# One operand item per half step, a second hand-out of side work in two MLP blocks, and other barriers inside the transform

## The chip, the cores and the metric

The kernel runs on one core of a Trainium2 chip. The metric is device time in microseconds of one launch; the median of three runs is given, and one further execution was recorded by the profiler. TensorE does the matrix products and transposes, VectorE and ScalarE move and combine what it leaves in PSUM, GpSimd and SyncE issue most transfers.

## The reference, cut to what matters

Three stages follow one another on `(4, 576, 512)` float32 data: attention with random features, a mixer (a token MLP and a channel MLP), and a block that adds a two-dimensional Fourier transform, normalizes and applies a second channel MLP.

```
# mixer, channel part; u has 4 x 576 rows of 512, w_ch1 is 512 x 1536
h2 = np.maximum(u @ w_ch1, 0.0) @ w_ch2
x = u + h2
# second block; w_ch1 is 512 x 2048
X = np.fft.fft(x, axis=1)
X = np.fft.fft(X, axis=2)
u = x + np.real(X)
mu = np.mean(u, axis=-1, keepdims=True)
var = np.mean((u - mu) ** 2, axis=-1, keepdims=True)
un = (u - mu) / np.sqrt(var + 1e-06)
out = u + np.maximum(un @ w_ch1, 0.0) @ w_ch2
```

## The kernel before

**Products.** Every operand is a sum of a high and a low part, and each product is three TensorE passes (high by high, high by low, low by high). A matmul has up to 512 columns.

**The first channel MLP** (`ch_block`, `mlp`) runs over five blocks of 512 rows, `at_` 0 to 4, in 12 steps each. A step is `up` (12 matmuls into a bank H, L775), `relu` (ScalarE writes hh, VectorE writes hl, L863 and L864) and `down` of the step before (12 matmuls into four banks A, L901). A block ends with eight additions on VectorE (L907).

**Side work.** Everything else is cut into items of a planned cost in microseconds and stands in two lists, `side.lead` and `side.rest`. `Side.step(budget)` adds its budget to a credit (at most 4.6), then hands out items from `lead` and after it from `rest` while the credit pays. A `None` is a barrier: it ends the list for this call. `side.later(fn, n)` puts an issue off by n calls. `side.until` takes items at once until a condition holds, whatever their cost. Handing out means that the instructions are written behind what has been written so far, in the queue of each engine; each engine then works through its own queue in that order. In `mlp` a step has one such call behind `down`, or with `twice` two with half the budget each, one ahead of `down` and one behind it. Before the change only the last MLP block `ff_block(0)` (matmuls L775 and L1285, 16 steps) has `twice`.

**What the lists hold.** From block 3 on, `lead` holds the transforms `dft(0)` to `dft(3)`, one for each batch. One transform is even0 to even4 (sums on VectorE; even4 ends with L983), s1e0 to s1e2 (matmuls L1055 to L1057 into a bank S, read out by `put`), odd0 to odd3, s1o0 to s1o2 (L1065, L1066; L1043 and L1044 read out the last), and for each of two row groups `both` (two banks S, L1082), plus and minus (`spectrum`, L1088 to L1090, read the two banks), and two nat (four transposes L1095 and one addition L1096 each), at last left0 and left1. There are two banks S, used in turn: whatever needs a third waits until the first has been read. `rest` holds the splitting of weights (`widen`: take, rest, size, high, low, unit, scaled at L371, then a store), in block 4 the first normalization `norm(0)` and the pair sums `sum_pairs`: eight times a load (L1222), `add` (L1227), `sums` (L1233 to L1236), a cast by ScalarE into a buffer `so` (L1242), `low` (L1246) and two stores (L420). Two buffers `so` serve in turn.

**Operand items.** When `rest` is empty, `begin_ff` opens the operands of the paired MLP, and the items of `prepare_early` (b11, b12, b22, b21, each for q = 0 and 1) transpose normalized rows `un` into a bank S (L1332) and split them (L1325, L1326).

**The paired MLP** (`paired_block`, L1507 and L1520) has eight steps of four products; `pace` hands out side work after each with a budget of 1.6 and a credit of at most 2.0, but not after the first two. Its second half, 16 slabs of nine matmuls, needs `reopen`, which stands in `lead` behind `dft(3)`: `side.until` forces it. From slab 4 on, it prepares the operands of the next paired block, which read the rows of `norm(2)` (stats L1165 and L1166, root, sqrt L1176, newton L1180 to L1185, `un` L1194); `side.until` forces those too.

Of the kernel before, what the change touches and what calls it, by code (L numbers as in the profile page):

```python
# [25 lines left out]
NCH, NFF = DCH // 128, DFF // 128  # L26
# [7 lines left out]

SLOT0_US, SLOT1_US, SLOT_US, FIRST_US, SHORT_US, CH_US, LAST_US, FF_US, S_US, SAVED_US = 1.2, 0.45, 1.2, 3.9, 1.2, 4.3, 4.9, 5.2, 1.6, 4.6


NP = NFF // 2  # L40
# [150 lines left out]
def pieces(t0, n):  # L191

    done = 0
    while done < n:
        b, s = divmod(t0 + done, S)
        step = min(n - done, S - s)
        yield done, step, b, s
        done += step
# [103 lines left out]
def mix_kernel(ctx: ExitStack, tc: tile.TileContext, qt, kt, va, om, w1, w2, wch, wff, t1, t2, out):  # L302
# [142 lines left out]
    def bank(tag):  # L445
        if tag not in pools:
            tag = "A"
        if tag == "A" and spare:

            tag = spare.pop(0)  # L450
            spare.append(tag)
        pl, bufs = pools[tag]
        return pl.tile([128, 512], F32, tag=tag, name=tag, bufs=bufs)
# [238 lines left out]
    for b in range(B):  # L692
# [4 lines left out]
        c = [("k", i, g) for i in range(kn, ke) for g in range(2)]  # L697
# [11 lines left out]
    early = []  # L709
# [18 lines left out]
    def turns(n, c):  # L728
        return list(range(n)) if c % 2 == 0 else list(range(n))[::-1]
# [19 lines left out]
    def halves(t, h):  # L749
        return t[:, 0, 512 * h:512 * h + 512], t[:, 1, 512 * h:512 * h + 512]  # L750
# [4 lines left out]
    def ch_cols(c):  # L755
        return min(BLK, NTOK - c * BLK)
# [12 lines left out]
    def up(w, uh, ul, n):  # L769

        hb = bank("H")
        c = 0
        for kk in range(4):
            for a, u in ((0, uh), (0, ul), (1, uh)):
                pe.matmul(out=hb[:, 0:n], lhsT=w(a, kk), rhs=u[:, kk, 0:n],  # L775
                          start=(c == 0), stop=(c == 11))
                c += 1
        return hb
# [81 lines left out]
    def relu(hb, n):  # L860
        hh = hp.tile([128, BLK], F32R, tag="hh", name="hh")[:, 0:n]
        hl = hp.tile([128, BLK], F32R, tag="hl", name="hl")[:, 0:n]
        act.activation(out=hh, in_=hb[:, 0:n], func=AF.Relu)  # L863
        dve.scalar_tensor_tensor(out=hl, in0=hb[:, 0:n], scalar=0.0, in1=hh, op0=ALU.max, op1=ALU.subtract)  # L864
        return hh, hl

    def mlp(steps, first_of, u, cols, down, budget, prepare, twice=False):


        prev = None  # L870
        for i, x in enumerate(steps):
            hb = mlp0.pop("hb") if "hb" in mlp0 else up(first_of(x), *u, cols)
            h = relu(hb, cols)
            last = i == len(steps) - 1
            if last:
                for fn in prepare[:1]:
                    fn()
            elif twice:
                side.step(budget / 2)
            if prev is not None:  # L880
                down(*prev)
            prev = i, x, h
            if not last:
                if fill:
                    fill.pop(0)()
                side.step(budget / 2 if twice else budget)
        for fn in prepare[1:]:
            fn()
        down(*prev)

    def ch_block(at_, c, u, prepare, budget):
        acc = [bank("A") for _ in range(4)]
        cols = ch_cols(c)

        def down(n, j, h):
            hi, lo = halves(mix.get(j), 1)
            hh, hl = h
            for c_, (a, v) in enumerate(((hi, hh), (lo, hh), (hi, hl))):
                for i in range(4):
                    cs = slice(i * 128, i * 128 + 128)  # L900
                    pe.matmul(out=acc[i][:, 0:cols], lhsT=a[:, cs], rhs=v, start=(n == 0 and c_ == 0),  # L901
                              stop=(n == NCH - 1 and c_ == 2))
            mix.used()
        mlp(turns(NCH, at_), ch_first, u, cols, down, budget, prepare)
        for i in range(4):
            for off, n, b, s in pieces(c * BLK, cols):
                dve.tensor_tensor(out=x2[b][:, i, s:s + n], in0=acc[i][:, off:off + n], in1=x2[b][:, i, s:s + n],  # L907
                                  op=ALU.add)

    u = mlp0["u"]  # L910
# [6 lines left out]
    u = u2  # L917
# [21 lines left out]
    U = [None] * B  # L939
# [7 lines left out]
    def dft(b):  # L947

        st = {}
        x = x2[b]  # L950
# [141 lines left out]
        def nat(u, src):  # L1092
            pb = bank("S")
            for c in range(4):
                pe.transpose(pb[:, c * 128:c * 128 + 128], src(c), ident)  # L1095
            dve.tensor_tensor(out=u, in0=pb, in1=u, op=ALU.add)  # L1096

        def rows(r):
            def both():
                if r == 0:  # L1100
                    U[b] = (xp if b else xu).tile([128, 4, 512], F32, tag="x2", name="U", padded_shape=[128, 4, S])
                e_ps, st["o"] = bank("S"), bank("S")
                stage2(e_ps, 0, st["ch"], 0, r)
                stage2(st["o"], 0, st["sh"], 1, r)
                st["e"] = f2.tile([128, 257], F32, tag="e", name="e", bufs=2)
                act.copy(out=st["e"], in_=e_ps[:, 0:257])

            def plus():
                spectrum(U[b][:, r], st["e"], st["o"], False)
                if r == 0:  # L1110
                    act.copy(out=st["e"][0:1], in_=st["alt"][:, 0:257])

            def minus():
                spectrum(U[b][:, 2 + r], st["e"], st["o"], True)

            return [(0.0, both), (0.9, plus), (0.9, minus),
                    None, (0.65, lambda: nat(U[b][:, r], lambda c: x[:, c, r:r + 256:2])),
                    (0.65, lambda: nat(U[b][:, 2 + r], lambda c: x[:, c, 288 + r:544 + r:2])), None]

        pr, po = b // 2, 64 * (b % 2)  # L1120

# [15 lines left out]
        def left1():  # L1137
            spectrum(L[pr][po:po + 64], st["e"][po:po + 64], st["o"][po:po + 64], False)
            if po:
                nat(L[pr], lambda c: gath[pr][:, c, :])  # L1140

        return ([(1.7, even0), (1.6, even1), (1.1, even2), (1.2, even3), (1.1, even4), None]
                + [(0.7, lambda: stage1e(0)), (0.7, lambda: stage1e(1)), None, (0.7, lambda: stage1e(2))]
                + [(1.4, odd0), (1.1, odd1), (1.1, odd2), (1.1, odd3), None]
                + [(0.7, lambda: stage1o(0)), (0.7, lambda: stage1o(1)), None, (0.7, lambda: stage1o(2)), None]
                + rows(0), rows(1) + [(0.8, left0), (1.5, left1)])

# [145 lines left out]
    big = {}  # L1293
    tmp = {}

    def half(c):
        return len(PAIRED[c]) // 2
# [72 lines left out]
    def late(k, q):  # L1370
        return temps(0)[2 * k + q]

    def prepare_early(q):

        n = 128 * half(0)
        xa = lambda: big["xa"][:, q * n:q * n + n]
        t3, t4 = (lambda: late(0, q)), (lambda: late(1, q))

        def b11():
            pb = turned(0, q, 0)
            act.copy(out=xa(), in_=pb)
            parts_of(0, P1, q, pb)

        def b12():
            pb = turned(0, q, 1)
            act.copy(out=t3(), in_=pb)
            dve.tensor_tensor(out=xa(), in0=pb, in1=xa(), op=ALU.subtract)
            parts_of(0, P5, q, xa())  # L1390

        def b22():
            pb = turned(0, q + 2, 1)
            dve.tensor_tensor(out=xa(), in0=pb, in1=xa(), op=ALU.subtract)
            dve.tensor_tensor(out=t3(), in0=pb, in1=t3(), op=ALU.subtract)
            parts_of(0, P6, q, xa())

        def b21():
            pb = turned(0, q + 2, 0)
            dve.tensor_tensor(out=t4(), in0=pb, in1=xa(), op=ALU.subtract)  # L1400
            parts_of(0, P2, q, pb)

        return [(0.7, b11), (1.2, b12), (1.7, b22), (1.2, b21)]
# [15 lines left out]
    for at_ in range(1, NBLK):  # L1419

        if at_ == 3:
            leave_slots()
            f2 = pf.enter_context(tc.tile_pool(name="f2", bufs=1, side="right", reuse_waits="tile"))
            right["n"] = pf.enter_context(tc.tile_pool(name="l3", bufs=2, side="right", reuse_waits="tile"))
        if at_ == 4:
            side.rest[0:0] = sum(norm(0), [])
            side.rest += sum_pairs()
        if at_ in (3, 4):
            side.lead += sum(dft(at_ - 3), [])
        v = operand()  # L1430
        last = at_ + 1 == NBLK
        ch_block(at_, BLOCKS[at_], u, ff_prepare(0, v) if last else [lambda: ch_split(BLOCKS[at_ + 1], v)],
                 SHORT_US if at_ == 1 else LAST_US if last else CH_US)
        u = v

    first_rows, later_rows = dft(2)
    stats, un = norm(1)
    side.lead.append((0.0, lambda: side.rest.__setitem__(slice(0, 0), stats[:-1])))
    side.lead += (first_rows + stats[-1:] + un + [None, (0.0, begin_ff)] 
                  + [x for both in zip(prepare_early(0), prepare_early(1)) for x in (*both, None)] + [(0.0, lambda: big.update(early=True))])  # L1440
    put = ff_block(0, u, [prepare_last, prepare_later], FF_US)
    side.drain()

# [211 lines left out]
```

## Time and profile before

| | |
|---|---|
| median of 3 runs | 950.37 us (949.04, 951.05, 950.37) |
| the profiled execution, its own time | 949.38 us |
| its span, first to last instruction | 947.6 us |
| TensorE, matmuls | 928.9 us busy (98%) |
| VectorE, ScalarE, GpSimd | 636.5, 303.6, 136.2 us busy |
| mean granted clock of TensorE | 0.996 |

All times of the trace count from the start of the span. A matmul's end in the trace is modelled and overlaps the next one; what a stream of matmuls costs is the distance from start to start. A wait in brackets behind a row is the time for which the engine stood idle ahead of it, and who ended it.

### The profile page before, as it was taken

The page shows a single profiled execution, that of the slowest core. Times are in us where ns is not written, and L with a number is a line of the kernel's source. Part 1 is how long each engine was busy: PE and PEld are TensorE (multiplying, and loading weights), DVE is VectorE, ACT ScalarE, POOL GpSimd, SP SyncE. Part 2 cuts the span into 40 slices and gives each one's busy share as a digit, 9 for nine tenths or more (in the row PEclk, how much of TensorE's full clock was granted, in tenths as well). Part 3 has the DMA queues.
Part 4 walks back from the last instruction along what each step waited for, and adds up shares of the span by engine and source line. Part 5 has one row for each costly group of instructions (what it writes and reads, how often), then busy time and mean ns, then how long its engine had stood idle before and what let it go on. Part 6 is the DMA issues. An engine that isn't in the chain of part 4 may idle for free.

```text
span 947.6 us, 13685 instructions
## 1 busy us (share of the span) xinstructions
PE 928.9 (98%) x5174; PEld 814.5 (86%) x5174; DVE 636.5 (67%) x1233; ACT 303.6 (32%) x688; POOL 136.2 (14%) x134
## 2 busy tenths in 40 slices
PE   9999999999999999999999899799999999999998
PEld 8999999988899888888888778589999888888886
DVE  5987999886775877877667778526666764233332
ACT  5986777722122222122212112312111251111120
POOL 3443435121211221020001002100000000000000
PEclk9999999999999999999999999899999999999999
DMA  8765564688896675672359559647665666565452
GB/s 273 240 215 190 179 222 151 254 316 322 323 423 275 223 256 210 222 274 81 133 189 412 199 187 340 227 145 254 228 227 192 208 209 210 185 208 187 158 196 105
DMA packets 61825, 214.36 MB, mean 226 GB/s; under 512 B 5568, under 2 KB 6208, under 8 KB 48064
## 3 DMA queue, kind: packets, MB, share of 16 engines
q1 hardware_dynamic: 51104, 153.52, 46.3%
q0 software_dynamic: 10512, 59.84, 17.0%
q8 instruction: 41, 0.67, 0.3%
q14 instruction: 24, 0.20, 0.1%
q10 hardware_dynamic: 144, 0.13, 0.0%
HBM read 167.20 MB, written 42.47 MB: 221 GB/s over the span
## 4 chain that ended last, share of the span: by engine, by line
PE 88%; DVE 5%; issue 3%; DMA 2%; ACT 1%; POOL 1%; SPq 0%; DVEq 0%; POOLq 0%; ACTq 0%
PE H L775 17%; PE A L1520 16%; PE A L901 15%; PE H L1507 14%; PE A L505 5%; PE H L539 4%; PE N L581 3%; PE A L1285 2%; PE A L564 2%; PE A L679 2%; PE A L666 1%; PE S L1082 1%; PE S L679 1%; PE S L1095 1%; DMA sw<-kept 1%
## 5 line engine op out<-in xcount | busy, mean ns | idle before, releaser
L775 PE MATMUL H<-uh,w 128*128 128x512 f32 (+1 forms) x608 | 189.0, 376 | 0.0
L775 PEld LDWEIGHTS H<-uh,w 128*128 128x128 f32 x608 | 111.9, 188 | 19.4
L863 ACT ACTIVATE hh<-H 128x512 fp32r<-128x512 f32 (+1 forms) x76 | 42.9, 564 | 231.2 <-PE H L775 231.0
L775 PE MATMUL H<-ul,w 128*128 128x512 f32 (+1 forms) x304 | 113.5, 373 | 0.4 <-DVE ul L762 0.4
L901 PE MATMUL A<-hh,w 128*128 128x512 f32 (+1 forms) x480 | 108.7, 369 | 0.0
L1507 PE MATMUL H<-b,w1t 128*128 128x384 f32 (+1 forms) x480 | 104.2, 363 | 0.0
L1507 PEld LDWEIGHTS H<-b,w1t 128*128 128x128 f32 x480 | 87.4, 188 | 11.5 <-DVE b L1326 0.4
L901 PEld LDWEIGHTS A<-hh,w 128*128 128x128 f32 x480 | 84.2, 188 | 15.0
L864 DVE SCALAR_TENSOR_TENSOR hl<-H,hh 128x512 fp32r<-128x512 f32 (+1 forms) x76 | 49.0, 644 | 50.9 <-ACT hh L863 50.7
L1520 PE MATMUL A<-w2t,hx 128*128 128x512 f32 x336 | 82.0, 392 | 0.0
L523 ACT ACTIVATE f<-A,mx 128x128 f32<-128x128 f32 x240 | 69.5, 397 | 23.2 <-DVE mx L519 22.8
L1520 PEld LDWEIGHTS A<-w2t,hx 128*128 128x128 f32 x336 | 62.5, 188 | 12.7
L775 PEld LDWEIGHTS H<-ul,w 128*128 128x128 f32 x304 | 57.3, 188 | 10.0 <-DVE ul L762 0.8
L901 PE MATMUL A<-hl,w 128*128 128x512 f32 (+1 forms) x240 | 59.2, 368 | 0.0
L901 PEld LDWEIGHTS A<-hl,w 128*128 128x128 f32 x240 | 42.6, 188 | 7.6
L519 DVE TENSOR_REDUCE mx<-A 128x4 f32<-128x512 f32 x70 | 47.4, 680 | 1.5 <-ACT f L523 0.9
L1520 PE MATMUL A<-w2t,hy 128*128 128x512 f32 x192 | 46.8, 389 | 0.0
L1520 PEld LDWEIGHTS A<-w2t,hy 128*128 128x128 f32 x192 | 36.0, 188 | 7.5
L539 PE MATMUL H<-v,f 128*128 128x65 f32 x320 | 40.2, 270 | 0.1
L359 DVE SCALAR_TENSOR_TENSOR cvo<-cvy,cvo 128x1024 int32<-128x1024 int32 (+2 forms) x32 | 39.7, 1240 | 0.5
L539 PEld LDWEIGHTS H<-v,f 128*128 128x128 f32 x320 | 38.9, 191 | 0.7 <-ACT f L527 0.3
L347 ACT ACTIVATE cvy<-cvy 128x1024 f32<-128x1024 f32 (+2 forms) x32 | 32.8, 1026 | 19.9 <-DVE cvy L340 19.8
(275 smaller groups left out, 1722.2 us busy)
## 6 DMA issues: line engine op xcount, KB each, us to landing
w<-kept SPq DMA_DIRECT2D x50, 1024.0 KB, 7.2
w2t<-kept SPq DMA_DIRECT2D x55, 512.0 KB, 4.3
w1t<-kept SPq DMA_DIRECT2D x48, 512.0 KB, 4.6
stg<-in_wff_dram POOLq DMA_DIRECT2D x16, 1024.0 KB, 6.8
kept<-cvo POOLq DMA_DIRECT2D x13, 1024.0 KB, 7.7
stg<-in_wch_dram SPq DMA_DIRECT2D x9, 1024.0 KB, 6.5
kept<-cvo POOLq DMA_DIRECT2D x16, 512.0 KB, 7.3
sw<-kept POOLq DMA_DIRECT2D x8, 1024.0 KB, 8.6
```

What stands on the lines that cost most here:

```text
L347: act.mul(out=st["y"], in_=st["y"], mul=2.0 ** -112)
L359: dve.scalar_tensor_tensor(out=st["h"], in0=st["y"].bitcast(I32), scalar=-0x80000000, in1=st["h"], op0=ALU.bitwise_and, op1=ALU.bitwise_or)
L505: pe.matmul(out=pj[:, p_ * 256:p_ * 256 + 256], lhsT=a[:, c, :], rhs=w, start=(n == 0), stop=(n == 2), skip_group_check=True)
L519: dve.tensor_reduce(out=mx, in_=p4, axis=AX.X, op=ALU.max, negate=True)
L523: act.activation(out=f[:, hh], in_=p4[:, hh], func=AF.Exp, bias=mx[:, hh])
L539: pe.matmul(out=kvp[b, g][:, hh * 65:hh * 65 + 65], lhsT=ft["k", i, g][:, hh, :], rhs=src["v", i, int(off > 0)][:, 4 * g + hh, :], start=( ...
L775: pe.matmul(out=hb[:, 0:n], lhsT=w(a, kk), rhs=u[:, kk, 0:n], start=(c == 0), stop=(c == 11))
L863: act.activation(out=hh, in_=hb[:, 0:n], func=AF.Relu)
L864: dve.scalar_tensor_tensor(out=hl, in0=hb[:, 0:n], scalar=0.0, in1=hh, op0=ALU.max, op1=ALU.subtract)
L901: pe.matmul(out=acc[i][:, 0:cols], lhsT=a[:, cs], rhs=v, start=(n == 0 and c_ == 0), stop=(n == NCH - 1 and c_ == 2))
L1507: pe.matmul(out=to, lhsT=w[:, a, cs], rhs=v[:, q], start=(start and n == 0), stop=(n == 5), skip_group_check=True)
L1520: pe.matmul(out=acc[t], lhsT=h[n // 2][:, t * 128:t * 128 + 128], rhs=w[:, n % 2], start=(begins and n == 0), stop=(ends and n == 2))
```

## The change

Five edits. The fourth and the fifth block of the first MLP (`at_` 3 and 4) call `side.step` twice a step with half the budget. Two budgets become smaller: `LAST_US`, that of block 4, and `FF_US`, that of the last MLP block. In the transform, the barriers behind even4, odd3, both and nat are doubled, while those behind s1e1, s1o1 and s1o2 stay single; `dft` is used for all four batches, so the doubled barriers also stand where a call comes once a step or once a product. The operand items, handed out in pairs between barriers, come one by one.

```
-..., CH_US, LAST_US, FF_US, S_US, SAVED_US = ..., 4.3, 4.9, 5.2, 1.6, 4.6
+..., CH_US, LAST_US, FF_US, S_US, SAVED_US = ..., 4.3, 4.7, 4.8, 1.6, 4.6

-    def ch_block(at_, c, u, prepare, budget):
+    def ch_block(at_, c, u, prepare, budget, twice=False):
-        mlp(turns(NCH, at_), ch_first, u, cols, down, budget, prepare)
+        mlp(turns(NCH, at_), ch_first, u, cols, down, budget, prepare, twice)

             return [(0.0, both), (0.9, plus), (0.9, minus),
-                    None, (0.65, ... nat ...), (0.65, ... nat ...), None]
+                    None, None, (0.65, ... nat ...), (0.65, ... nat ...), None, None]

-        return ([(1.7, even0), ..., (1.1, even4), None]
+        return ([(1.7, even0), ..., (1.1, even4), None, None]
                 + [(0.7, lambda: stage1e(0)), (0.7, lambda: stage1e(1)), None, (0.7, lambda: stage1e(2))]
-                + [(1.4, odd0), ..., (1.1, odd3), None]
+                + [(1.4, odd0), ..., (1.1, odd3), None, None]
                 + [(0.7, lambda: stage1o(0)), (0.7, lambda: stage1o(1)), None, (0.7, lambda: stage1o(2)), None]

         ch_block(at_, ...,
-                 SHORT_US if at_ == 1 else LAST_US if last else CH_US)
+                 SHORT_US if at_ == 1 else LAST_US if last else CH_US, at_ > 2)

     side.lead += (first_rows + stats[-1:] + un + [None, (0.0, begin_ff)]
-                  + [x for both in zip(prepare_early(0), prepare_early(1)) for x in (*both, None)] + ...)
+                  + [x for both in zip(prepare_early(0), prepare_early(1)) for fn in both for x in (fn, None)] + ...)
```

## Rows read from the trace of the kernel before

**Rows 1.** The page: busy us (share of the span) xinstructions of each engine.

```profile
PE   928.9 (98%) x5174; PEld 814.5 (86%) x5174; DVE 636.5 (67%) x1233; ACT 303.6 (32%) x688; POOL 136.2 (14%) x134
```

**Rows 2.** TensorE's waits: line, releaser, us in total, times, longest.

```profile
PE S L1332 <- DVE b L1326: 5.2, 1, 5.2
PE S L1095 <- ACT le L1135: 1.8, 1, 1.8
...
PE S L1082 <- DVE U L1096: 1.1, 1, 1.1
...
PE S L1056 <- DVE fo L983: 0.8, 1, 0.8
...
PE S L1066 <- DVE fo L983: 0.4, 1, 0.4
```

**Rows 3.** Order of time around the operand items: start, us, engine, line, tiles.

```profile
595.53 0.82 PE L1332 MATMUL S<-ident,un 128*128 128x128 f32 x6
...
597.36 1.06 ACT L1242 CAST so<-cvy 128x1024 fp32r<-128x1024 f32 x1 [7.15 <-DMA kept<-so]
...
604.29 1.54 PE L1332 MATMUL S<-ident,un 128*128 128x128 f32 x6 [5.21 <-DVE b L1326]
```

**Rows 4.** Stretches: length, busy of PE, PEld, DVE, ACT, POOL, granted clock, DMA.

```profile
526.50:533.20 6.70, 3.78 (x29) 3.31 (x28) 4.39 (x13) 2.01 (x3) 0.00 (x0) 1.00 0.57 238
...
595.53:618.51 22.98, 17.00 (x73) 13.57 (x72) 13.77 (x25) 8.49 (x16) 3.01 (x4) 0.85 0.48 176
605.40:609.60 4.20, 4.20 (x13) 3.33 (x12) 0.56 (x1) 0.36 (x1) 0.00 (x0) 0.50 0.87 345
```

**Rows 5.** Order of time: the start of block 3, and of the third transform.

```profile
386.29 1.98 PE L901 MATMUL A<-hh,w 128*128 128x512 f32 x8
...
387.01 0.36 DVE L983 COPY fo<-fo 128x297 f32<-128x297 f32 x1
...
545.34 0.49 PE L1056 MATMUL S<-t_sb,fo 128*128 128x129 f32 x2 [0.81 <-DVE fo L983]
```

**Rows 6.** Order of time in block 4 around the first sum; landing of these loads.

```profile
490.92 1.23 DVE L371 SCALAR_TENSOR_TENSOR cvo<-cvo,cvy 128x1024 fp32r<-128x1024 f32 x1
...
492.06 0.68 DVE L864 SCALAR_TENSOR_TENSOR hl<-H,hh 128x512 fp32r<-128x512 f32 x1
...
492.98 1.07 POOL L1222 DMA_DIRECT2D sw<-kept  x2
...
494.67 0.48 DVE L1044 SCALAR_TENSOR_TENSOR sh<-sh,t_sb,S 93x258 fp32r<-93x258 f32 x1
...
500.30 1.23 DVE L1227 TENSOR_TENSOR cvy<-sw 128x1024 f32<-128x1024 f32 x1 [5.14 <-DMA sw<-kept]
...
504.75 0.42 DVE L1088 TENSOR_TENSOR U<-e,S 128x257 f32<-128x257 f32 x1 [0.79 <-ACT e L1106]
...
507.06 0.72 PE L1095 MATMUL S<-ident,x 128*128 128x128 f32 x4 [0.51 <-DVE U L1090]
...
DMA to landing us min/median/max: 7.3/8.6/11.7
```

**Rows 7.** Order of time in the paired MLP, up to slab 4.

```profile
728.50 0.69 DVE L1165 BATCH_NORM_STATS2 sts<-U 128x6 f32<-128x512 f32 x1
...
729.44 0.69 DVE L1165 BATCH_NORM_STATS2 sts<-U 128x6 f32<-128x512 f32 x1
...
743.43 8.32 PE L1520 MATMUL A<-w2t,hx 128*128 128x512 f32 x36
...
744.23 1.02 DVE L1513 SCALAR_TENSOR_TENSOR hx<-t,hx 128x384 fp32r<-128x384 f32 x2
...
745.17 0.20 DVE L1180 RECIPROCAL y<-y 128x8 f32<-128x8 f32 x1
...
746.21 1.46 DVE L1194 TENSOR_SCALAR un<-U,mv,y 128x512 f32<-128x512 f32 x3
...
751.59 0.60 PE L1332 MATMUL S<-ident,un 128*128 128x128 f32 x4
```

More of the change, by code (lines that the diff above doesn't have):

```diff
@@ L33 @@
 BLOCKS = [0, NBLK - 1, *range(1, NBLK - 1)]
-SLOT0_US, SLOT1_US, SLOT_US, FIRST_US, SHORT_US, CH_US, LAST_US, FF_US, S_US, SAVED_US = 1.2, 0.45, 1.2, 3.9, 1.2, 4.3, 4.9, 5.2, 1.6, 4.6
+SLOT0_US, SLOT1_US, SLOT_US, FIRST_US, SHORT_US, CH_US, LAST_US, FF_US, S_US, SAVED_US = 1.2, 0.45, 1.2, 3.9, 1.2, 4.3, 4.7, 4.8, 1.6, 4.6
 NP = NFF // 2
@@ L1116, in rows @@
             return [(0.0, both), (0.9, plus), (0.9, minus),
-                    None, (0.65, lambda: nat(U[b][:, r], lambda c: x[:, c, r:r + 256:2])),
-                    (0.65, lambda: nat(U[b][:, 2 + r], lambda c: x[:, c, 288 + r:544 + r:2])), None]
+                    None, None, (0.65, lambda: nat(U[b][:, r], lambda c: x[:, c, r:r + 256:2])),
+                    (0.65, lambda: nat(U[b][:, 2 + r], lambda c: x[:, c, 288 + r:544 + r:2])), None, None]
         pr, po = b // 2, 64 * (b % 2)
@@ L1140, in left1 @@
                 nat(L[pr], lambda c: gath[pr][:, c, :])
-        return ([(1.7, even0), (1.6, even1), (1.1, even2), (1.2, even3), (1.1, even4), None]
+        return ([(1.7, even0), (1.6, even1), (1.1, even2), (1.2, even3), (1.1, even4), None, None]
                 + [(0.7, lambda: stage1e(0)), (0.7, lambda: stage1e(1)), None, (0.7, lambda: stage1e(2))]
-                + [(1.4, odd0), (1.1, odd1), (1.1, odd2), (1.1, odd3), None]
+                + [(1.4, odd0), (1.1, odd1), (1.1, odd2), (1.1, odd3), None, None]
                 + [(0.7, lambda: stage1o(0)), (0.7, lambda: stage1o(1)), None, (0.7, lambda: stage1o(2)), None]
@@ L1439, in mix_kernel @@
     side.lead += (first_rows + stats[-1:] + un + [None, (0.0, begin_ff)]
-                  + [x for both in zip(prepare_early(0), prepare_early(1)) for x in (*both, None)] + [(0.0, lambda: big.update(early=True))])
+                  + [x for both in zip(prepare_early(0), prepare_early(1)) for fn in both for x in (fn, None)] + [(0.0, lambda: big.update(early=True))])
     put = ff_block(0, u, [prepare_last, prepare_later], FF_US)
```

## The prediction

> **What bounds the kernel now.** I read the page's busy line first: TensorE is busy 98% of a span of 947.6 us [rows 1]. Its matmul stream is therefore the bound, and 18.7 us of idle are all that a reordering can win directly. Second, the list of waits says who ended that idle time [rows 2]. Nearly all of it lies in the stretch that the change touches: 5.2 us until VectorE had freed a PSUM bank for the operand items of the last block, and 5.0 us in smaller waits inside the transforms (1.8, 1.1, 0.8, two of 0.4, and the 0.5 of [rows 6]). Third, the order in time: at 595.53 the pair b11 goes out, the next pair wants the same two banks at 599.1, and VectorE frees them only at 604.3. It is behind because ScalarE had sat 7.15 us before it until a store from buffer `so` landed, and the pair sums queued behind that cast [rows 3]. Fourth, the stretches: the granted clock is 0.50 after that wait and 1.00 around the smaller ones [rows 4].
>
> A program's order follows from `Side.step` by arithmetic: add the budget, cap it at 4.6, take items while the credit pays, stop at a `None`. I worked this through the list for both versions; for the kernel before, each transform group then falls between the same matmul groups as in the trace. I write 5 A for the call of step 5 ahead of `down`, 5 B for the one behind it; blocks 3 and 4 are those with `at_` 3 and 4.
>
> **What is removed.**
> *Operand items.* 595.53 to 618.51 took 22.98 us [rows 4]. It holds 48 matmuls of 512 columns, at 0.227 each (36 in 8.16 us, [rows 7]) 10.9 us, and 24 transposes at about 0.11, 2.7 us. So 9.4 us are lost, some 2.3 of them in the half-speed stretch (4.20 us at 0.50 is worth 2.1, and the transposes ahead of it a little). After: the last `low` of the pair sums falls in half step 7 B instead of 10 A, because the half steps of blocks 3 and 4 hand out more of them; b11 starts at 9 A instead of 10 B; and each bank is wanted again after a whole step. Three half steps (8 us) lie where one lay, which covers the backlog. I take 9.4 as gained; if the cover failed, up to 9.4 would return.
> *Waits in the second and third transform.* The 5.0 us of smaller waits, and 0.1 to 0.2 of restart for each: 6.0. The places change, so all go; what takes their place follows.
>
> **What is added.**
> *Start of blocks 3 and 4.* Before, even0 to even4 go out in two steps and s1e0 a step later. Now s1e0 stands in half step 2 A. VectorE cannot start sooner, because the eight final additions and hl come first: in block 3 the last instruction of even4 (L983) ends at 387.37 already now, and TensorE is at 386.29 where the group will stand [rows 5]. L1056 needs L983, as 545.34 shows [rows 5]: 0.9 us of wait in each block, 0.9 in the last MLP as now, and about 0.45 there when s1e2 follows s1e0 by half a step. Together 3.15. Bounds: 0 and, if the first `None` pair gave nothing, 5.
> *Block 4, the first sum.* Before, the loads of the pair sums go out in step 6 with credit 0.08 left, and the first `add` a step later. Now half step 5 A begins with 1.2 + 2.35 = 3.55: s1o2 0.7, `scaled` 1.22, its store and both loads 0, and 1.63 is left, which pays for `add` (1.2) at once. VectorE then stands at L1227 until the load lands, and queued behind it are both spectra, hl and the sums. In the trace the load is issued 0.83 after `scaled` ends (490.92 + 1.23) and L1227 starts 7.32 after that; TensorE's second nat group starts 2.31 after the spectra begin (504.75 to 507.06) and waits for exactly them [rows 6]. From the start of the s1o2 group: hl, the two copies behind s1o2 and `scaled`, about 3.1 (0.4 + 0.6 + 0.9 + 1.2, from [rows 6]); 0.8; 7.3; `add` 1.25; 2.3: the bank is free at 14.75. TensorE gets there after three MLP halves (2.72 each), 0.4, both0 1.0 and the first nat 0.45: 9.95. Wait 4.8. Bounds: 0 if the load were there, 6.1 at the median landing of 8.6, 9.2 at the longest, 11.7. I take 4.8 since the same load took 7.3 there. Another 0.35 is lost before s1o2, where newton, four `un`, `low` and `unit` fill one half step, and 0.1 at left1.
> *The paired MLP.* It paces the rest of the transforms with 1.6 a call, 30 calls in all before its second half. dft(3) and the rest of dft(2) hold eight more `None`. Before, `reopen` comes at call 25; now nat1 of dft(3) comes at call 30, and left0, left1 and `reopen` are forced out by `side.until`: 0.3 us for a bank. The second normalization, which was done before slab 0, now starts there, two `stats` per slab, and at slab 4 `side.until` forces sqrt, newton and eight `un` right before the transposes that read them. VectorE from the start of slab 0: additions 0.8, relu parts 0.94 (two), eight `stats` at 0.9 (728.50, 729.44: 0.94 for one pair), three more relu parts 1.4, root and sqrt 0.6, newton 1.04, four `un` at 0.46 [rows 7]: 14.0. TensorE reaches the transposes after 36 matmuls, 8.16. Wait 5.6 (0.2 of their own work overlaps). Bounds: 0 and 7.
> *Twice, budgets, other barriers.* The same matmuls in the same number; transposes now come in eight groups of three for four of six. I take 0, covered by the 0.1 a group costs. Loads of weights keep their places. Side work and DMAs that move earlier are the pair sums: their loads and stores are issued by GpSimd up to three steps sooner, beside the weights that SyncE fetches; in the rows their landing takes 7.3 to 11.7 [rows 6], and by my count no later sum comes sooner than that behind its load.
> *The clock.* An idle stretch of 5.2 us was followed by 0.50 of the clock; 6.7 us with 2.9 us of idle in two waits kept 1.00 [rows 4]. The two new waits, 4.8 and 5.6, are near the first. Each may cost 2.3 or nothing. I take one of the two.
> The page "TensorE: Matmul & The Clock Gate" of the Trainium skill (Part 1, What's actually happening) says that "the default state is throttled, and activity releases the throttle"; by it both waits would be followed by the lower level of 1.2 GHz. The trace bears it out at the one long wait, and not at the shorter ones.
>
> **Sum.** Gone 9.4 + 6.0 = 15.4. New 3.15 + 4.8 + 0.45 + 0.3 + 5.6 = 14.3 (the wait for L983 in the last MLP stands in both sums). Clock 2.3. Net +1.2 us on the profiled execution's 949.38 (span 947.6 and 1.8 around it): 950.6. That execution lies 1.0 below the median of 950.37, so 951.6 against the median.
>
> **Rivals**, against the median. A measurement of this kernel (949.04 to 951.05) can tell about 0.2% from no change: 948.5 to 952.3 is "the same".
> *Forecast*: both new waits come, one costs the clock: 951.6. Chance 0.35, and 0.12 more for neither costing it, 949.3.
> *Both cost the clock*: 951.6 + 2.3 = 953.9, and 955.2 if the load also takes its median 8.6. The 0.50 after the only long wait speaks for it. 0.22. Slower. It is the case that the Trainium skill's page on the clock gate, named above, would have.
> *The wait for the first sum is hidden*: decided at the load, which would have to land within 2.5 us of its issue, or `add` would have to fall a step later; 951.6 - 4.8 - 1.2 (half a clock price): 945.6. Against it: 5.14 us of VectorE's idle at the same instruction already now [rows 6]. 0.12. Faster.
> *The paired MLP keeps up*, with 30 calls enough or the normalization early enough: 951.6 - 5.9 - 1.1, likewise: 944.6. Decided at call 30. 0.06. Both hidden: 938, the full gain, 0.07. Faster.
> *The operand items still wait*: if the sums still trail at half step 9 A, up to 9.4 comes back: 956 to 961. Three half steps between speak against it. 0.06. Slower.
>
> **How the numbers follow.** Predicted 951.6, the likeliest. Range 943.5 to 957.0: it leaves out the full gain and the return of the operand wait, with the tails about 0.18. Faster: 0.25 of the hidden cases and a little of the forecast's own spread, 0.27. Same: 0.40. Slower: 0.33. The forecast's own range is 948 to 954.
>
> **What would show it.** Right: in the waits L1332 behind VectorE's b is gone from the last MLP but stands, with `un` (L1194) as releaser, at the slab of the paired MLP; L1095 waits some 5 us behind U (L1090) in block 4, with L1227 idle for 8 us behind the load; two waits near 0.9 behind L983 in blocks 3 and 4; left0 and left1 of the fourth transform after the last pace. Wrong: L1227 without idle, no wait at slab 4, or the operand wait still there. Most likely to break the sum: the landing time of one load, and whether the clock falls.

## The result and the profile after

The changed kernel is slower. Its first four runs took 960.24 us in the median (956.59 to 964.09) beside 950.01 for the kernel before: a ratio of 1.0108, 95% interval 1.006 to 1.0156. In the profiled one of those four (964.09) TensorE ran at half speed at the start of the attention, in code that the change does not touch (last section); one more took 962.63, and no trace of it was kept. Run again, with a profile that lacks that stretch, it took 957.08 (956.49 to 957.98) beside 950.81: 1.0066, interval 1.0051 to 1.0081. I take this second figure, some 6.3 us, as what the change costs. 951.6 was forecast, "the same"; the time lies outside the range at either figure, by little at the second.

The page of the kernel after, its busy line:

```profile
PE   936.8 (97%) x5174; PEld 821.5 (85%) x5174; DVE 635.6 (66%) x1233; ACT 304.8 (32%) x688; POOL 134.5 (14%) x134
```

The instructions are as many as in [rows 1]; TensorE is busy 8 us longer for the same 5174 matmuls, so part of what this execution lost is clock. TensorE's waits in the same profile (line, releaser, us in total, times, longest):

```profile
PE S L1095 <- DVE U L1090: 9.4, 1, 9.4
PE S L1332 <- DVE un L1194: 4.2, 1, 4.2
PE S L1056 <- DVE fo L983: 2.4, 3, 0.8
PE H L539 <- ACT f L523: 1.7, 1, 1.7
...
PE S L1082 <- DVE U L1096: 0.3, 1, 0.3
```

Against [rows 2], L1332 behind b is gone, and so are 1.8 behind le and 0.4 behind L983 at L1066; L1056 waits three times in place of one. The two large entries are block 4's first sum, where [rows 6] has 0.51, and slab 4 of the paired MLP, which is new. Every place for which a wait above half a microsecond was forecast is in the list, and in the transforms and MLPs no other new one is.

Where the time went, by three stretches with the same matmuls in both kernels: from the first MLP's first product to the last MLP's first down product, from there to the first product of the paired MLP, and from there to the last matmul. Length, busy time of PE, PEld, DVE, ACT, POOL, granted clock, DMA share and GB/s. The kernel before:

```profile
187.75:535.98 348.23, 343.37 (x1770) 293.41 (x1769) 256.69 (x459) 80.09 (x144) 48.34 (x60) 1.00 0.69 261
535.98:638.23 102.25, 94.64 (x438) 77.98 (x437) 66.87 (x135) 23.53 (x44) 10.67 (x15) 0.97 0.61 218
638.23:943.13 304.90, 304.75 (x1487) 263.53 (x1485) 149.96 (x291) 57.94 (x112) 0.00 (x0) 1.00 0.59 196
```

The kernel after, in its second profile (957.98 us, span 956.2):

```profile
187.43:546.44 359.01, 345.99 (x1771) 295.17 (x1769) 265.50 (x474) 81.82 (x146) 50.94 (x66) 0.99 0.70 264
546.44:638.43 91.99, 91.18 (x437) 75.56 (x436) 57.97 (x121) 21.81 (x42) 6.56 (x9) 1.00 0.56 199
638.43:951.70 313.27, 308.66 (x1487) 265.53 (x1485) 150.24 (x291) 58.30 (x112) 0.00 (x0) 0.99 0.58 191
```

The middle stretch gives 10.3 back, the expected gain. The first loses 10.8 and the last 8.4. With -0.3 ahead of them that is +8.6 between the two profiles, while the medians differ by 6.3: the profile of before lies 1.4 under the median of its runs here, that of after 0.9 over its own.

Block 4 around the first sum, in order of time, the first profile of after:

```profile
492.37 1.22 DVE L371 SCALAR_TENSOR_TENSOR cvo<-cvo,cvy 128x1024 fp32r<-128x1024 f32 x1
493.73 0.32 SPq L737 DMA_DIRECT2D w<-kept  x1
493.88 0.55 POOL L413 DMA_DIRECT2D kept<-cvo  x1 [41.22 <-DVE cvo L371]
494.42 1.07 POOL L1222 DMA_DIRECT2D sw<-kept  x2
506.57 1.23 DVE L1227 TENSOR_TENSOR cvy<-sw 128x1024 f32<-128x1024 f32 x1 [12.99 <-DMA sw<-kept]
510.01 1.10 PE L1095 MATMUL S<-ident,x 128*128 128x128 f32 x4 [9.41 <-DVE U L1090]
```

In [rows 6] the load went out at 492.98 and L1227 started 7.3 later. Here it is 12.15 from issue to use, with VectorE idle for 13.0. What differs is the second row: a weight fetch of 1 MB goes out 0.15 us ahead of the store and 0.7 ahead of the loads. They stand in different queues. The store goes when `scaled` (L371) has ended, at 493.59, and the loads behind it; SyncE's fetch waits for matmuls of `down` (L901) that end at about the same time. So the order in which they were written does not decide which goes first: the half step that writes the store and the loads, 5 A, is written ahead of the `down` behind which the fetch stands. In the kernel before, the fetch nearest to it came later than the loads:

```profile
493.77 0.32 SPq L734 DMA_DIRECT2D w<-kept  x1
```

What each queue moved between the issue and 498.4 us (q1 carries SyncE's fetches, q0 GpSimd's stores and loads; packets, MB, share of the engines), after and then before:

```profile
q1 hardware_dynamic: 105, 0.86, 83.8%
```

```profile
q0 software_dynamic: 224, 1.70, 91.8%
```

Each is the only data queue listed in its stretch, from 494.0 after and from 493.0 before. In both, what was issued first moved alone, and in the kernel after the store and the loads stood still while 0.86 of the fetch's 1 MB moved. From 498.5 to 506.0 both queues moved, 2.25 MB on q0 and 0.72 on q1.

The paired MLP at slab 4, the same profile of after:

```profile
756.77 2.43 PE L1520 MATMUL A<-w2t,hx 128*128 128x512 f32 x10
763.36 1.75 PE L1332 MATMUL S<-ident,un 128*128 128x128 f32 x4 [4.17 <-DVE un L1194]
764.77 4.19 PE L1520 MATMUL A<-w2t,hx 128*128 128x512 f32 x9
```

[rows 7] has 36 matmuls in 8.32 and four transposes in 0.60; here nine take 4.19 and the four 1.75. The clock (the column after POOL's) in the stretches behind the two waits, second profile:

```profile
502.90:507.70 4.80, 4.80 (x15) 3.80 (x14) 4.70 (x8) 1.04 (x1) 0.68 (x2) 0.53 0.41 160
758.10:762.90 4.80, 4.80 (x15) 3.83 (x15) 2.71 (x6) 1.50 (x3) 0.00 (x0) 0.50 0.00 0
```

Both waits cost the clock: 1.2 in place of 2.4 GHz for some 4.5 us each, about 2.1 us of time each (the twelve L775 matmuls behind the first took 4.65 from the first start to the last, 502.98 to 507.63; the next twelve took 2.50).

### The profile page after: what moved, and what is told of

Its sections match the earlier page's. It is cut to its first block, busy times and chain, and to the rows that moved or that the text cites. A ratio compares the mean times of both kernels' runs of the same rounds, so it can differ in the third digit from the quotient of the medians.

```text
span 962.3 us, 13678 instructions
## 1 busy us (share of the span) xinstructions
PE 936.8 (97%) x5174; PEld 821.5 (85%) x5174; DVE 635.6 (66%) x1233; ACT 304.8 (32%) x688; POOL 134.5 (14%) x134
## 4 chain that ended last, share of the span: by engine, by line
PE 87%; DVE 9%; DMA 1%; ACT 1%; issue 1%; POOL 0%; DVEq 0%; ACTq 0%; POOLq 0%
PE H L775 18%; PE A L1520 15%; PE A L901 14%; PE H L1507 14%; PE A L505 4%; PE A L1285 4%; PE H L539 3%; PE N L581 3%; PE A L666 1%; PE S L1082 1%; PE A L564 1%; DMA sw<-kept 1%; PE A L679 1%; PE S L1332 1%; PE S L679 1%
## 5 line engine op out<-in xcount | busy, mean ns | idle before, releaser
L775 PE MATMUL H<-uh,w 128*128 128x512 f32 (+1 forms) x608 | 189.3, 377 | 0.0
L775 PEld LDWEIGHTS H<-uh,w 128*128 128x128 f32 x608 | 112.4, 189 | 19.7
L775 PE MATMUL H<-ul,w 128*128 128x512 f32 (+1 forms) x304 | 113.9, 375 | 0.4 <-DVE ul L762 0.4
L901 PE MATMUL A<-hh,w 128*128 128x512 f32 (+1 forms) x480 | 109.2, 370 | 0.0
L901 PEld LDWEIGHTS A<-hh,w 128*128 128x128 f32 x480 | 83.9, 188 | 14.8
L523 ACT ACTIVATE f<-A,mx 128x128 f32<-128x128 f32 x240 | 69.4, 392 | 22.1 <-DVE mx L519 21.7
L775 PEld LDWEIGHTS H<-ul,w 128*128 128x128 f32 x304 | 57.6, 189 | 10.0 <-DVE ul L762 0.8
L901 PE MATMUL A<-hl,w 128*128 128x512 f32 (+1 forms) x240 | 59.2, 369 | 0.0
L901 PEld LDWEIGHTS A<-hl,w 128*128 128x128 f32 x240 | 42.6, 188 | 7.6
L539 PE MATMUL H<-v,f 128*128 128x65 f32 x320 | 43.6, 284 | 1.7 <-ACT f L523 1.7
L539 PEld LDWEIGHTS H<-v,f 128*128 128x128 f32 x320 | 42.7, 207 | 1.9 <-ACT f L523 1.9
L363 DVE SCALAR_TENSOR_TENSOR cvo<-cvo,stg 128x1024 f32<-128x1024 int32 (+2 forms) x32 | 39.8, 1243 | 0.0
```

Source lines behind the costliest of these rows:

```text
L363: dve.scalar_tensor_tensor(out=st["l"].bitcast(F32), in0=st["l"], scalar=2.0 ** 32, in1=st["lw"].bitcast(U32), op0=ALU.mult, op1=ALU.add)
L523: act.activation(out=f[:, hh], in_=p4[:, hh], func=AF.Exp, bias=mx[:, hh])
L539: pe.matmul(out=kvp[b, g][:, hh * 65:hh * 65 + 65], lhsT=ft["k", i, g][:, hh, :], rhs=src["v", i, int(off > 0)][:, 4 * g + hh, :], start=( ...
```

## The experiments

All compute the whole reference. Experiments 1 to 4 ran beside a kernel before of 950.70, experiments 5, 6, 8 and 9 beside 950.81, and 7, 10 and 11 beside 950.01. "Below after" is counted from the 957.08 of experiment 6.

**1. The first load earlier.** The first load of the pair sums goes to the front of the side list:

```
-            side.rest[0:0] = sum(norm(0), [])
-            side.rest += sum_pairs()
+            pairs = sum_pairs()
+            side.rest[0:0] = pairs[:1] + sum(norm(0), [])
+            side.rest += pairs[1:]
```

> Changed kernel, but the first load of the pair sums goes to the front of the side list, so that it is issued some seven half steps before the add that reads it; nothing else moves. Theory (TensorE's 9.4 us behind U in block 4 are VectorE standing at the add until this load lands, and the wait costs the clock as well): that wait goes to under 1 us, 9.4 and about 2 of half-speed time come back, about 948.5 us against 960.2. Rival (groups of the transform a half step apart are too close, whatever VectorE does): the wait shrinks little or moves to the next group, above 955 us. Second rival (the load is slow because pair sums now run beside the weights): it lands late here too, and the second sum waits instead: 952 to 956 us.

951.09 us (949.94 to 954.52), ratio 0.9999 (0.9979 to 1.0018): 6.0 below after. The first load went out 40.8 us ahead of its add (at 485.42), the second load stood behind a fetch and landed late, as the first does in the kernel after:

```profile
444.60 0.55 POOL L1222 DMA_DIRECT2D sw<-kept  x1
498.88 1.23 DVE L1227 TENSOR_TENSOR cvy<-sw 128x1024 f32<-128x1024 f32 x1 [5.04 <-DMA sw<-kept]
```

Its waits:

```profile
PE S L1332 <- DVE un L1194: 4.2, 1, 4.2
PE S L1095 <- DVE gath L1130: 2.4, 1, 2.4
PE S L1056 <- DVE fo L983: 2.4, 3, 0.8
...
PE S L1095 <- DVE U L1090: 0.9, 1, 0.9
```

The wait for U falls from 9.4 to 0.9; 2.4 comes at the left rows, because the second add now stands behind the second load: of the second rival the wait came, though a small one, and the time lies just under its range. So the load, and not VectorE's other work, held block 4.

**2. Single barriers late.** The second half of the third transform and the whole of the fourth get single `None`s back:

```
+        gaps = [None] * (1 if b == 3 else 2), [None] * (1 if b >= 2 else 2)
...
-                    None, None, (0.65, lambda: nat(U[b][:, r], lambda c: x[:, c, r:r + 256:2])),
+                    *gaps[r], (0.65, lambda: nat(U[b][:, r], lambda c: x[:, c, r:r + 256:2])),
```

> Changed kernel, but the barriers of the fourth transform and of the second row group of the third are single again, as before the change: eight None fewer in the paired MLP. Theory (the eight None push reopen and the second normalization past the 30 calls, and forcing them makes TensorE wait for un at slab 4): the wait for un (4.2 us, with what follows 5.3) and 0.5 at left0 go, and with them one half-speed stretch of about 2: 952 to 953 us against 960.2. Rival (the wait at slab 4 comes of VectorE being busier late in the paired MLP for other reasons): it stays, 959 to 961 us.

949.39 us (948.68 to 951.28), ratio 0.9975 (0.9954 to 0.9996): 7.7 below after. Slab 4 and the left rows of the fourth transform no longer wait and the clock stays:

```profile
740.00:770.00 30.00, 30.00 (x146) 24.87 (x145) 21.16 (x43) 12.96 (x28) 0.00 (x0) 1.00 0.65 221
```

The eight extra `None`s are what made the second normalization late.

**3. Both repairs.**

> Both edits of the two runs beside it. Theory (two waits with their two half-speed stretches are all that the change costs, and the rest of it gains 15 us): 938 to 942 us, faster than before by about 1%. Rival (half steps in blocks 3 and 4 cost by themselves): no faster than 948 us.

944.24 us (941.25 to 951.24), ratio 0.9928 (0.9904 to 0.9953). The two repairs nearly add up: 6.0 + 7.7 from 957.08 would be 943.4. The rival (no faster than 948) falls, and the range of the theory, 938 to 942, was missed by 2: a wait of 3.6 at the left rows of block 4 was left. The profile is of the longest of the ten runs, 951.24, which has the half-speed stretch of the last section.

**4. The operand items alone.** The kernel before with one operand item to a half step and nothing else:

```
-                  + [x for both in zip(prepare_early(0), prepare_early(1)) for x in (*both, None)] + [(0.0, lambda: big.update(early=True))])
+                  + [x for both in zip(prepare_early(0), prepare_early(1)) for fn in both for x in (fn, None)] + [(0.0, lambda: big.update(early=True))])
```

> Kernel before, with only the operand items handed out one to a half step. Theory (the wait of 5.2 us for a bank is VectorE's backlog behind the pair sums; spacing alone gives it two half steps instead of one): of the 9.4 us about 2 stay, no half-speed stretch, 942 to 946 us against 950.0. Rival (spacing only puts the wait off, since the backlog is what it was): 948 to 951 us.

944.90 us (942.98 to 951.48), ratio 0.9934 (0.9906 to 0.9962). One wait of 1.1 is left of the 5.2 behind b, and no lower clock:

```profile
604.89 0.55 PE L1332 MATMUL S<-ident,un 128*128 128x128 f32 x3 [1.06 <-DVE b L1326]
```

This one line of the change brings 5.8 us by itself. Added to this kernel, the rest of the change costs 12 (957.08 for 944.90).

**5. The weight fetch later.** The kernel after, with one fetch of block 4 issued a step later:

```
-            mix.used()
+            if at_ == 4 and n == 4:
+                mix.at += 1
+            else:
+                mix.used()
```

> The kernel after, and one weight fetch of block 4 (the one that is issued in step 5, at 493.73, 0.15 us ahead of the store and 0.7 ahead of the loads of the pair sums) is issued one step later, some 6 us behind them. Nothing else is moved. Theory (the first load lands late because a weight fetch of 1 MB now goes out ahead of it and takes the DMA engines first): issue to landing falls from 12.15 us to 7.3 to 8.5, as it was in the kernel before, VectorE's idle time at the first add from 13.0 to 8 to 9, and TensorE's wait for U from 9.6 to 4.5 to 6; the time falls by 4 to 5 us. Rival (the store of 1 MB and the two loads that GpSimd issues together are what fills the DMA engines, whatever SyncE does): landing stays at 11 to 12.5 and the wait at 9 to 10.

952.50 us (951.76 to 954.07), ratio 1.002 (1.0009 to 1.003): 4.6 below after. The load goes out at 487.62:

```profile
487.62 0.55 POOL L1225 DMA_DIRECT2D sw<-kept  x1
494.75 1.22 DVE L1230 TENSOR_TENSOR cvy<-sw 128x1024 f32<-128x1024 f32 x1 [7.96 <-DMA sw<-kept]
498.19 1.07 PE L1098 MATMUL S<-ident,x 128*128 128x128 f32 x4 [4.40 <-DVE U L1093]
```

and the stretch behind that wait:

```profile
498.20:503.00 4.80, 4.80 (x16) 4.01 (x17) 4.70 (x9) 1.04 (x1) 0.02 (x1) 0.64 1.01 423
```

The moved fetch went out at 493.34. With it out of the way, 7.1 us from issue to use and a wait of 4.4: in the kernel after the load stood behind the fetch, and the rival (store and loads fill the engines by themselves) falls. A wait of 4.4 is still followed by a clock of 0.64.

**6. The kernel after once more.**

> The kernel after as it is, once more. In its first profiled run a half-speed stretch of 13.7 us stood at the start of the attention, whose code the change does not touch; two of its four runs took 962.6 and 964.1, two 956.6 and 957.8. Theory (that stretch comes and goes by itself, in the kernel before as well, and is no part of the change): the runs without it take 956 to 958 and are most of them, so that the change itself costs 6 to 8 us; the median lies nearer 957 than 962. Rival (the change brings it on): most runs take 962 to 965.

957.08 us, all four runs between 956.49 and 957.98. The same kernel has the lower clock in the attention in one profile and not in the other, so it is no fixed cost of the change. Of the 31 runs of the kernel before beside experiments 1 to 4, three took 955.6 to 958.4; whether they had the same stretch is not shown, since no trace of them was kept.

**7. Operand items in pairs again.** The kernel after without the line of experiment 4:

> The kernel after with its operand items in pairs again, two to a half step, as before the change; all else as after (957 us). Theory (the gain of 9.4 us comes from the spacing: two items in one half step want the same two banks again before VectorE has cleared them): TensorE's wait for b comes back with 2 to 5 us, with lower clock behind it if it is long, 959 to 966 us. Rival (it comes from the pair sums, which blocks 3 and 4 now hand out three half steps earlier, so that VectorE has no backlog when the operand items come): no wait for b above 0.5 us, 956 to 958 us.

957.98 us (957.22 to 959.41), ratio 1.0075 (1.0057 to 1.0093). No wait for b; the only one in the operand items is this:

```profile
608.99 0.52 PE L1332 MATMUL S<-ident,un 128*128 128x128 f32 x3 [0.38 <-DVE tmp L1395]
```

The rival holds: in the kernel after, the operand wait is gone without the spacing. The reason that the rival gives shows in the last `low` of the pair sums (L1246). Here it comes 6.5 us ahead of b11, and in the kernel before 7.0 behind it (b11 at 595.53, [rows 3]). First experiment 7, then the kernel before:

```profile
591.41 1.23 DVE L1246 TENSOR_TENSOR so<-cvy,so 128x1024 fp32r<-128x1024 f32 x1
597.94 0.82 PE L1332 MATMUL S<-ident,un 128*128 128x128 f32 x6
```

```profile
602.54 1.23 DVE L1246 TENSOR_TENSOR so<-cvy,so 128x1024 fp32r<-128x1024 f32 x1 [0.56 <-ACT so L1242]
```

Experiment 4 says that the spacing alone does nearly the same. They are two remedies for one wait, so their gains do not add: without the spacing the rest of the change costs 8.0 (957.98 beside 950.01), and the spacing then brings about 1, which is within the spread.

**8 to 11. Towards a faster kernel.** From experiment 3: the second add half a step later (its cost 3.2 for 1.2); then a third `None` between even4 and s1e0 in blocks 3 and 4; then a `None` between the left items of block 4; then the third `None` in the last MLP's transform too (b < 3 in place of b < 2).

```
-                items.append((1.2, lambda p=p: add(p)))
+                items.append((3.2 if p == 1 else 1.2, lambda p=p: add(p)))
...
-        return ([(1.7, even0), (1.6, even1), (1.1, even2), (1.2, even3), (1.1, even4), *gaps[0]]
+        return ([(1.7, even0), (1.6, even1), (1.1, even2), (1.2, even3), (1.1, even4), *gaps[0], *([None] if b < 3 else [])]
...
-                + rows(0), rows(1) + [(0.8, left0), (1.5, left1)])
+                + rows(0), rows(1) + [(0.8, left0), *([None] if b == 1 else []), (1.5, left1)])
```

> The kernel with both repairs (first load early, single barriers in the second half of the third transform and in the fourth), and the second add of the pair sums costs 3.2 in place of 1.2, so that it falls a half step later. Theory (the 3.7 us that TensorE still waits at the left rows of block 4 are VectorE's 4.4 us at the second add, behind a load that takes 12 us, and nothing else): VectorE's idle time there falls to 0 to 2 and TensorE's wait at the left rows to below 1; 940 to 941.5 us. Rival (the left rows wait for VectorE because too much is queued there, whatever the load does): a wait of 2 to 4 us stays within the same group or the next, and the time stays at 943 to 945.

942.88 us (941.25 to 944.54), ratio 0.9916 (0.9898 to 0.9934). The wait at the left rows falls from 3.6 to 0.9, but 1.5 and 1.3 stand in the last MLP behind the even items, where 0.8 stood: the theory on the second load holds, and the time lies 1.4 above its range, for which the new waits and a lower clock behind them (last section) are the likely reason.

> The same, and a third None between even4 and s1e0 in the transforms of blocks 3 and 4, so that s1e0 falls a half step later there. Theory (the two waits of 0.9 behind L983 are a matter of place: VectorE needs 0.9 us more than two half steps give): both waits go, two of 0.9 in all; 938 to 940 us. Rival (VectorE is what limits the start of the transform, so that a wait of the same size comes at the next group, s1o0 or the first sum): the time is that of the kernel with two barriers, within 0.5 us.

942.23 us (941.67 to 944.44), ratio 0.9913 (0.9896 to 0.9931). Both of the waits behind L983 in blocks 3 and 4 (0.75 and 0.81 in experiment 8) went, and this one came at the left rows of block 4:

```profile
513.83 1.12 PE L1096 MATMUL S<-ident,gath 128*128 128x128 f32 x4 [3.19 <-ACT le L1136]
```

So the places were as theory had them, and the time as the rival had it, though not for the rival's reason: a cast behind a store was late next.

> The kernel with the third barrier (942.2), and a None between the two left items of block 4's transform. There ScalarE's cast of a pair sum stands 5.4 us until a store from its buffer has landed, the copy to le is queued behind that cast, and TensorE waits 3.2 us for it. Theory (a matter of place): the second left item falls a half step of 2.7 us later, and 0 to 0.7 us of the 3.2 are left; 938.5 to 940 us. Rival (ScalarE is held up by the store however late the item is): 2 to 3 us of wait stay and the time is 941 to 942.5.

938.56 us (937.19 to 944.83), ratio 0.9893 (0.9847 to 0.9939); of the 3.2 a wait of 0.2 is left, as theory said.

> The same, with the third None also in the transform of the last MLP, where two waits of 1.5 and 1.3 us behind VectorE's even items were left. Theory: both go, 1.5 to 3 us less than the kernel before it in this list, 936 to 938.5 us, if nothing at the paired MLP comes later. Rival: the operand items or the second normalization are pushed late and wait, 0 to 4 us more than it.

937.08 us (935.83 to 941.62), ratio 0.9867 (0.9835 to 0.9899). 1.3 behind the even items shrank to 0.3, and in place of the other 1.5 a wait of 1.4 came at another place, behind ch; the time is in the theory's range, but the step from 938.56 is within the spread, so neither theory is decided. As a whole this kernel is some 13 us faster than before and 20 faster than after.

## Why the prediction was wrong

**What bounds the kernel** and **the order of the side work** were right: each large new wait stood at the group and behind the releaser that were named.

**Operand items.** 9.4 forecast as gained; the middle stretch is 10.3 shorter, which includes small waits of the transform there. Of the reasons given, earlier sums and wider spacing, either takes most or all of the wait away (experiments 4 and 7).

**Start of blocks 3 and 4.** 0.9 a block forecast; 0.9 and 1.0 lost from start to start, and about 1.0 in the last MLP, each some 0.16 more than the wait in the list, which bears out the restart of 0.1 to 0.2 that the prediction adds to a wait. Right. The two small terms, 0.45 at s1e2 and 0.35 before s1o2, have no wait in the list.

**The first sum: the step that failed.** "I take 4.8 since the same load took 7.3 there." The formula was right; the landing time put into it was not. (Its terms for TensorE add up to 10.0 and not 9.95, which changes nothing.) With the load landing as in the kernel before, the wait is 4.4 (experiment 5). But the load's new place changed more than the distance to its add: where the nearest fetch of SyncE had been issued 0.8 behind it, one was now issued 0.7 ahead. The load took 12.15, the wait 9.4 and, in the second profile, 10.0. The text had the pieces ("beside the weights that SyncE fetches") and even a bound of 9.2 for the longest landing; "Loads of weights keep their places" looks at each queue by itself; it did not ask which of two queues would issue first.

**The paired MLP.** 5.6 at slab 4 forecast; 4.2, and about 1.0 more in the transposes that ran at the lower clock. 0.3 for the bank at the left rows: 0.3. The place and the cause were right, as experiment 2 shows; the wait was forecast 1.4 too long. (Its parts for VectorE add up to 13.8 and not 14.0, so 5.4 follows from them.)

**The clock: the second term that was too small.** "I take one of the two." The clock fell behind both, 2.1 us each: 0.53 and 0.50 behind waits of 10.0 and 4.2, and 0.64 behind 4.4 in experiment 5. By the page "TensorE: Matmul & The Clock Gate" of the Trainium skill (Part 1, What's actually happening), for which the throttled level is the default state, both would have been taken; at these two waits the traces agree with it.

**The sum mended.** 1.2, and 5.2 for the wait (10.0 for 4.8), and 1.9 for the clock (4.2 for 2.3): +8.3, where the two profiles differ by 8.6. That they agree so closely is partly luck: the smaller misses (1.4 less wait and 1.0 more in the transposes at slab 4, the two small terms, 10.3 for 9.4 in the middle stretch, which holds other waits too) were left as they are. The rival that came is "Both cost the clock", with the first wait at more than its upper bound.

**What stays open.** Twice and the new budgets were not run without the other barriers, so their share of the 12 us is not known by itself. The late barriers (7.7) and the place of the first load (6.0) account for all of it and a little more. The place of that load comes from twice, the barriers and the budgets together, and which of them put it just behind the fetch was not tried.

## What to carry to other kernels

When an edit moves a step forward, list the transfers of every queue near its new place and write down which is issued first afterwards. The written order does not say it: each queue goes on when what it waits for is done. Here a load that comes 0.7 us behind a 1 MB fetch instead of 0.8 ahead of it lands 5 us later. Put a load several steps ahead of its use rather than in the step that uses it. And try the parts of a change one at a time, from both ends: here one line brings 5.8 us alone and about 1 beside the other parts, which take the same wait away and cost more elsewhere.

## What the runs showed of the hardware

**The clock falls behind shorter waits than the kernel before suggested.** In the MLPs and transforms a wait of 2.4 was followed by 0.62 (experiment 1, left rows), while [rows 4] has 1.00 with 2.9 us of idle time in two waits. The stretch behind the 2.4:

```profile
517.00:521.50 4.50, 4.50 (x16) 3.65 (x16) 1.29 (x4) 0.00 (x0) 0.39 (x1) 0.62 1.01 420
```

**The same waits are not always followed by the same clock.** Experiments 8 and 9 both have waits of 1.46 and 1.27 at the start of the transform in the last MLP. Behind them the clock was 0.50 in the profile of experiment 8 and 1.00 in that of experiment 9, so the length of a wait alone does not settle it. First 8, then 9:

```profile
543.50:545.00 1.50, 1.50 (x7) 1.30 (x6) 1.47 (x4) 0.40 (x1) 0.00 (x0) 0.50 0.00 0
```

```profile
543.00:546.00 3.00, 3.00 (x20) 2.62 (x19) 2.90 (x9) 0.78 (x2) 0.00 (x0) 1.00 0.00 0
```

**The start of the attention runs at half speed in some executions.** The same 15 us (24 to 39), first the kernel before, then the first profile of after, where TensorE had waited 1.7 for f (L523) at 24.1:

```profile
24.00:39.00 15.00, 14.96 (x129) 14.65 (x129) 14.79 (x31) 13.19 (x39) 5.33 (x4) 1.00 0.77 234
```

```profile
24.00:39.00 15.00, 14.90 (x75) 14.90 (x76) 9.90 (x18) 9.34 (x29) 3.32 (x3) 0.54 0.65 176
```

75 matmuls in place of 129: some 8 us lost by the start of the first MLP (195.69 for 187.75). Experiment 3 had the same after a wait of 1.7 and experiment 11 after 1.5, with a clock of 0.54 and 0.66; experiment 5 waited 1.1 at the same line and kept 1.00. That the wait brings it on is what these profiles suggest, and no run was made to show it.
